# Attention shares: one VectorE multiply over spread reciprocals in place of four scalings on two engines

## The chip, the cores and the metric

The kernel runs on one core of a Trainium2 chip. The metric is the device time of one execution in microseconds; lower is better.

## What is computed

The reference is a chain of three layers in float32 over 4 sequences of 576 tokens:

- attention with 8 heads of 64, a causal window of 128 keys and a distance bias: `scores = scale * q k^T + bias`, then `attn = exp(scores - max)`, `attn = attn / (sum(attn) + 1e-9)`, `out = attn v`;
- a feed-forward layer with layer norm: `x + relu(norm(x) * g_ln @ w_ch1) @ w_ch2`, 512 to 2048 to 512;
- a gated layer with a convolution over three tokens: `h = relu(x @ w_in)`, `h * sigmoid(conv(h)) @ w_out`, 512 to 1024 to 512.

The change touches the division of `attn` by its sums. All weights arrive as 64-bit floats and are turned into float32 parts on the chip.

## The kernel before, in words

The work has an attention stage, whose order is written out by hand, and everything after it, whose order a planner in the program (`Plan`, lines 24 to 210) makes from due times and costs. The change touches the attention stage alone.

Attention works on 72 tiles (two pairs of sequences, four pairs of heads, nine tiles of 128 queries), each with two heads. A step of the code handles a pair of tiles, so four score blocks of 128 x 128; there are 36 pairs. The loop at line 835 takes two pairs, `a` and `b`, a round, 18 rounds in all. Each engine runs its instructions in the order in which the loop writes them, and semaphores tie the engines together. What a pair passes through:

- `scores` (line 692): TensorE, into PSUM. Each query tile sees two key tiles.
- `join` and `minima` (lines 720 and 726): VectorE, a masked copy (L724) that lays the two key tiles' halves over each other, and a minimum per row (L728). Both read PSUM.
- `exponentials` (line 730): ScalarE, four calls (L738), each also writing its row's sum into `sm`.
- `shares` (line 743): VectorE adds 1e-9 to the four sums (L746) and takes reciprocals (L747), and then the four 128 x 128 blocks of `pp` are scaled in place (L750). Blocks 0 and 2 are done by VectorE, blocks 1 and 3 by GpSimd.
- `turn_p` (line 755): four TensorE transposes of `pp` into PSUM (L760).
- `copy_p` (line 762): ScalarE copies them to SBUF (L765).
- `select_p` (line 768): GpSimd makes the parts of the two key tiles, two selects of 128 x 512 (L772).
- `values` (line 777): TensorE multiplies with `v` (L788), and `outputs` (line 793) copies the result out.

In a round the VectorE queue holds: join and minima of `a`, join and minima of `b`, `shares(b - 4)`, the extras of the even half round, `shares(a)`, the extras of the odd one. GpSimd's holds: `select_p(b - 8)`, its part of `shares(b - 4)`, extras, its part of `shares(a)`, `select_p(a - 4)`, extras.

The extras (`extras`, line 817) are mostly the conversion of the first twelve feed-forward weight blocks (`weights_step`, line 373; `FINE_START` and `FINE_AT` say when): a rescale on GpSimd (L341), three integer steps on VectorE (L349, L354, L359), a copy on ScalarE (L388) and a subtraction on VectorE (L391). By their half rounds L354 falls between the two `shares` of a round, and L391, L359 and L349 behind the second. A few rounds also carry a layer norm's steps, among them four subtractions on GpSimd (L483). Behind the loop the last pairs are drained with their own written order (lines 894 to 917).

Of the kernel before, what the change touches and what calls it, by code (L numbers as in the profile page):

```python
# [14 lines left out]
ALU = mybir.AluOpType  # L15
PSUM = bass.MemoryType.PSUM

P = 128
# [176 lines left out]
def tile_kernel(  # L195
# [28 lines left out]
    V, S, G, T = nc.vector, nc.scalar, nc.gpsimd, nc.tensor  # L224
# [288 lines left out]
    with ExitStack() as actx:  # L513
# [110 lines left out]
        def blhs_f(kind: int, a: int = 0):  # L624
            return blhs[:, kind, a:].bitcast(F32)

        V.tensor_scalar(
            out=blhs[:, 0, :], in0=cf[:, P:W], scalar1=er[0], scalar2=er[1], op0=ALU.mult, op1=ALU.add
        )
        V.tensor_scalar(out=cb[:, 3:4], in0=er[0], scalar1=-1.0, scalar2=None, op0=ALU.mult)  # L630
        for i, r, base in ((1, 2, 3), (2, 3, 3), (0, 4, 1)):
            V.scalar_tensor_tensor(
                out=cb[:, i : i + 1], in0=er[r], scalar=BIG, in1=cb[:, base : base + 1],
                op0=ALU.mult, op1=ALU.add,
            )
        for i in range(4):
            cs = slice(i * D, (i + 1) * D)
            V.tensor_scalar(
                out=b0[:, cs], in0=cf[:, cs], scalar1=er[1], scalar2=cb[:, i : i + 1],
                op0=ALU.mult, op1=ALU.add,  # L640
            )
        for kind, r in ((1, 2), (3, 4)):
            V.tensor_scalar(
                out=blhs[:, kind, :], in0=blhs_f(0), scalar1=er[r], scalar2=None, op0=ALU.add
# [3 lines left out]
            out=blhs[:, 2, TAIL:], in0=blhs_f(0, TAIL), scalar1=er[2], scalar2=er[3],  # L648
            op0=ALU.add, op1=ALU.add,
        )  # L650
        for pr in range(NPAIR):
            V.tensor_scalar(
                out=brhs[:, pr, :], in0=b0, scalar1=sl[:, pr : pr + 1], scalar2=None, op0=ALU.mult
# [89 lines left out]
        def shares(n: int):  # L743

            sm = live["sm", n]
            V.tensor_scalar(out=sm[:, 1], in0=sm[:, 0], scalar1=1e-9, scalar2=None, op0=ALU.add)  # L746
            V.reciprocal(out=sm[:, 1], in_=sm[:, 1])  # L747
            pp = live["pp", n].rearrange("p u h j -> p (u h) j")
            for i in range(4):
                (G if i % 2 else V).tensor_scalar(  # L750
                    out=pp[:, i, :], in0=pp[:, i, :], scalar1=sm[:, 1, i : i + 1], scalar2=1.0,
                    op0=ALU.mult, op1=ALU.mult,
                )

        def turn_p(n: int, pool=ps_t, tag="pt"):
            pp = live.pop(("pp", n))
# [78 lines left out]
        for n in range(0, NS, 4):  # L835
# [21 lines left out]
            if n > 4:  # L857
                shares(b - 4)
# [4 lines left out]
            exponentials(a)  # L863
            exponentials(b, range(2 if 0 < n and not last else 4))
            shares(a)
            if not before:
                shares(b)
# [1006 lines left out]
```

## Time and profile before

| what | value |
|---|---|
| time, median of 3 runs | 740.08 us (736.44 to 740.39) |
| the profiled execution | 737.25 us, of which its span is 735.6 us |
| PE, DVE, ACT, POOL busy in the span | 97%, 73%, 55%, 30% |
| attention stage | from the start to about 148 us |

PE is TensorE, PEld its weight loads, DVE VectorE, ACT ScalarE, POOL GpSimd, SP SyncE; L750 is line 750 of the kernel. Busy time of an engine is a union of its instructions' recorded times. On VectorE the recorded time of one instruction runs some 0.08 us into that of the next, so the distance from start to start is what an instruction takes of the queue.

### The profile page before, as it was taken

The numbers are of one execution on the slowest core, as the hardware profiler recorded it, in microseconds if no ns is written. First come the engines' busy times: TensorE is split into PE (matmuls) and PEld (weight loads), VectorE is DVE, ScalarE is ACT, GpSimd is POOL, SyncE is SP. The second block draws the span as 40 slices with busy tenths as digits, with TensorE's granted clock in tenths as the row PEclk, the third lists the DMA queues.
The fourth block names the chain that finished last, engine by engine and source line by source line (L and its number), as shares of the span: only waits on it lengthen the run. The fifth ranks groups of instructions, "written<-read, shape, count | busy, mean of one in ns | idle before, by whom it ended". The sixth has DMA issues, their size and how long they took to land.

```text
span 735.6 us, 13436 instructions
## 1 busy us (share of the span) xinstructions
PE 711.3 (97%) x4704; PEld 664.1 (90%) x4704; DVE 534.2 (73%) x1073; ACT 404.4 (55%) x1050; POOL 223.3 (30%) x388
## 2 busy tenths in 40 slices
PE   7999998899999999999999999999999999999998
PEld 6777776799889999999999999999999898998887
DVE  6899999578899845655678765568369988787630
ACT  4888877635444323333436333344377787776741
POOL 1778789635542312321210233243421000000000
PEclk9999999999999999999999999999999999999999
DMA  6877765226859714987870599997832000000011
GB/s 152 185 180 175 199 159 144 71 86 201 241 164 336 260 52 121 290 256 247 244 225 25 155 283 296 297 270 227 255 93 80 16 16 29 29 30 15 29 53 48
DMA packets 122302, 114.62 MB, mean 156 GB/s; under 512 B 63552, under 2 KB 87292, under 8 KB 122236
## 3 DMA queue, kind: packets, MB, share of 16 engines
q1 hardware_dynamic: 101020, 76.81, 35.1%
q0 software_dynamic: 20160, 36.71, 18.5%
q8 instruction: 37, 0.61, 0.3%
q10 hardware_dynamic: 1056, 0.26, 0.2%
q14 instruction: 29, 0.24, 0.1%
HBM read 80.70 MB, written 33.05 MB: 155 GB/s over the span
## 4 chain that ended last, share of the span: by engine, by line
PE 67%; DVE 2%; DMA 1%; ACT 1%; POOL 1%; issue 0%; SPq 0%; ACTq 0%
PE bank L1008 66%; DMA fa<-in_moe_w_out 1%; DVE fa L978 1%; DMA fa<-in_moe_w_ch 1%; PE bank L1055 1%; DVE fa L986 0%; POOL r L1183 0%; ACT fa L971 0%; DVE fa L359 0%; DVE x L978 0%; ACT fa L339 0%; DVE h L1698 0%; DVE fa L354 0%; ACT L971 0%; POOL small L1077 0%
## 5 line engine op out<-in xcount | busy, mean ns | idle before, releaser
L1008 PE MATMUL bank<-hhr,r 128*128 128x384 f32 x1152 | 214.8, 338 | 2.9 <-DVE hhr L986 1.0
L1008 PE MATMUL bank<-r,r 128*128 128x288 f32 (+1 forms) x1248 | 203.9, 314 | 1.6 <-DVE fa L978 0.9
L1008 PEld LDWEIGHTS bank<-hhr,r 128*128 128x128 f32 x1152 | 198.7, 188 | 5.3 <-POOL r L1183 1.6
L1008 PEld LDWEIGHTS bank<-r,r 128*128 128x128 f32 x1248 | 194.0, 188 | 4.4 <-ACT fa L971 1.4
L1279 POOL DMA_DIRECT2D r<-w1d x96 | 51.4, 536 | 164.7 <-PE bank L1008 146.8
L971 ACT ACTIVATE fa<-bank 128x288 f32<-128x288 f32 (+1 forms) x112 | 49.9, 445 | 67.4 <-PE bank L1008 65.5
L1008 PE MATMUL bank<-r 128*128 128x512 f32 (+2 forms) x360 | 80.7, 369 | 0.0
L1008 PEld LDWEIGHTS bank<-r 128*128 128x128 f32 x360 | 64.1, 188 | 9.0
L1008 PE MATMUL bank<-xn,r 128*128 128x384 f32 x360 | 67.3, 336 | 0.0
L971 ACT ACTIVATE r<-fa 128x256 fp32r<-128x256 f32 (+2 forms) x94 | 47.7, 521 | 33.0 <-DVE fa L359 11.5
L1008 PEld LDWEIGHTS bank<-xn,r 128*128 128x128 f32 x360 | 62.8, 188 | 0.0
L971 ACT ACTIVATE hhr<-bank 128x384 fp32r<-128x384 f32 x46 | 22.5, 490 | 73.1 <-PE bank L1008 73.1
L978 DVE TENSOR_TENSOR fa<-bank,fa 128x288 f32<-128x288 f32 (+1 forms) x88 | 43.5, 500 | 24.3 <-ACT fa L971 14.4
L738 ACT ACTIVATE pp<-ps,mn 128x128 f32<-128x128 f32 x144 | 51.3, 380 | 13.1 <-DVE mn L728 9.6
L750 POOL TENSOR_SCALAR pp<-pp,sm 128x128 f32<-128x128 f32 x72 | 43.2, 611 | 32.8 <-DVE sm L747 31.6
L986 DVE SCALAR_TENSOR_TENSOR fa<-fa,cw 128x576 f32<-128x576 f32 x64 | 51.2, 813 | 1.5 <-ACT fa L971 0.7
L978 DVE TENSOR_TENSOR r<-fa,r 128x256 fp32r<-128x256 f32 (+1 forms) x74 | 37.6, 521 | 16.7 <-ACT r L971 13.4
L772 POOL TENSOR_SCALAR_AFFINE_SELECT pt<-pc 128x512 f32<-128x512 f32 x72 | 46.9, 680 | 1.7 <-ACT pc L765 1.4
L713 PE MATMUL ps<-kt,qt 64*128 64x256 f32 x288 | 43.9, 399 | 2.5 <-ACT pp L738 1.7
L788 PE MATMUL po<-pt,rawv 128*64 128x128 f32 x544 | 38.4, 283 | 6.9 <-POOL pt L772 4.4
L1008 PE MATMUL bank<-r,hhr 128*128 128x512 f32 (+1 forms) x192 | 44.5, 381 | 0.0
L788 PEld LDWEIGHTS po<-pt,rawv 128*64 128x64 f32 x544 | 29.5, 138 | 15.5 <-POOL pt L772 12.2
(136 smaller groups left out, 1062.4 us busy)
## 6 DMA issues: line engine op xcount, KB each, us to landing
r<-w1d POOLq DMA_DIRECT2D x96, 256.0 KB, 4.8
fa<-in_moe_w_ch SPq DMA_DIRECT2D x32, 512.0 KB, 4.6
w1d<-r SPq DMA_DIRECT2D x40, 256.0 KB, 3.3
wind<-r SPq DMA_DIRECT2D x28, 256.0 KB, 4.1
r<-wind POOLq DMA_DIRECT2D x28, 256.0 KB, 4.2
out<-h SPq DMA_DIRECT2D x17, 256.0 KB, 2.0
rawq<-in_q SPq DMA_DIRECT2D x32, 128.0 KB, 3.8
rawv<-in_v SPq DMA_DIRECT2D x32, 128.0 KB, 3.0
```

What stands on the lines that cost most here:

```text
L713: T.matmul(ps[:, h, u, :].rearrange("p (o j) -> p o j", o=2), lhs, rhs, start=i == 0, stop=i == 1,)
L738: S.activation(pp[:, u, h, :], sc[:, h, u], AF.Exp, bias=mn[:, h, u : u + 1], scale=-1.0, accum_out=sm[:, 0, i : i + 1],)
L750: (G if i % 2 else V).tensor_scalar(out=pp[:, i, :], in0=pp[:, i, :], scalar1=sm[:, 1, i : i + 1], scalar2=1.0, op0=ALU.mult, op1=ALU.mult,)
L772: G.affine_select(out=parts[:, i], in_=pc, compare_op=ALU.is_ge, fill=0.0, base=base, pattern=[[0, 4], [sign, P]], channel_multiplier=-sign,)
L788: T.matmul(po[h * D : (h + 1) * D, u, :], rvs[bl, pr][:, t - 1 + i, h, :], pt[:, i, 2 * u + h, :], start=i == i0, stop=i == 1,)
L971: "S", ns + 90 * isinstance(scale, bass.AP), lambda: S.activation(out, src, func, **kw),
L978: "V", tt_ns(cols(out)), lambda: V.tensor_tensor(out=out, in0=a, in1=b, op=op),
L986: lambda: V.scalar_tensor_tensor(out=out, in0=a, scalar=sc, in1=b, op0=op0, op1=op1),
L1008: T.matmul(out, lhs, rhs, start=start and n == 0, stop=stop and n == len(items) - 1, skip_group_check=True,)
L1055: T.transpose(px[:, c, :], xs[c], ident)
L1279: plan.add("G", 1100, lambda: nc.gpsimd.dma_start(dst, src), [src], [dst], nbytes=262144)
```

## The change

In `shares` the loop of four scalings is replaced by one VectorE multiply over all four blocks, 128 x 512. Its second operand is the row of four reciprocals, each read 128 times by a step of zero. GpSimd has no part in `shares` any more. The sums, the reciprocals and everything else stay.

```diff
             V.tensor_scalar(out=sm[:, 1], in0=sm[:, 0], scalar1=1e-9, scalar2=None, op0=ALU.add)
             V.reciprocal(out=sm[:, 1], in_=sm[:, 1])
             pp = live["pp", n].rearrange("p u h j -> p (u h) j")
-            for i in range(4):
-                (G if i % 2 else V).tensor_scalar(
-                    out=pp[:, i, :], in0=pp[:, i, :], scalar1=sm[:, 1, i : i + 1], scalar2=1.0,
-                    op0=ALU.mult, op1=ALU.mult,
-                )
+            r = sm[:, 1].rearrange("p (i o) -> p i o", o=1).broadcast_to([P, 4, P])
+            V.tensor_tensor(out=pp, in0=pp, in1=r, op=ALU.mult)
```

## Rows read from the trace of the kernel before

**Rows 1.** Windows: stretch, length; busy time and count per engine; clock; DMA share, GB/s.

```profile
core 0 of [0], span 735.6 us
...
27.59:131.23 103.64, 96.83 (x1006) 77.87 (x1006) 97.19 (x226) 85.60 (x344) 85.08 (x134) 0.98 0.69 168
131.23:147.84 16.61, 14.35 (x142) 11.72 (x139) 8.46 (x22) 9.26 (x31) 10.22 (x18) 1.00 0.25 78
147.84:213.13 65.29, 62.05 (x362) 60.15 (x361) 55.51 (x89) 31.18 (x59) 31.87 (x31) 1.00 0.56 167
```

**Rows 2.** Chain that ended last, in order of time: start us, us, what.

```profile
213.13 4.09 PE bank L1008 x22
```

**Rows 3.** Groups on VectorE up to 143 us: count, busy us, mean ns, idle before.

```profile
L750 DVE TENSOR_SCALAR pp<-pp,sm 128x128 f32<-128x128 f32 x72 | 25.5, 396 | 1.3
...
L746 DVE TENSOR_SCALAR sm<-sm 128x4 f32<-128x4 f32 x36 | 7.0, 195 | 1.8 <-ACT pp L738 1.8
L349 DVE TENSOR_SCALAR fa<-fa 128x512 int32<-128x512 int32 x12 | 6.8, 566 | 0.6 <-POOL fa L341 0.6
```

**Rows 4.** Groups on GpSimd up to 143 us, the same columns.

```profile
L772 POOL TENSOR_SCALAR_AFFINE_SELECT pt<-pc 128x512 f32<-128x512 f32 x72 | 46.9, 680 | 1.7 <-ACT pc L765 1.4 <-PE po L788 0.4
L750 POOL TENSOR_SCALAR pp<-pp,sm 128x128 f32<-128x128 f32 x72 | 43.2, 611 | 32.8 <-DVE sm L747 31.6 <-ACT kt L814 0.5 <-ACT pc L765 0.4
```

**Rows 5.** Waits of VectorE from 27 to 143 us: total us, times, longest.

```profile
DVE ps L724 <- PE ps L713: 3.6, 6, 1.2
DVE fa L349 <- POOL fa L341: 0.6, 1, 0.6
```

**Rows 6.** Waits of TensorE up to 143 us.

```profile
PE po L788 <- POOL pt L772: 4.4, 6, 1.3
```

**Rows 7.** Timeline of VectorE in one round: start us, us, instruction, count.

```profile
65.07 0.60 DVE L750 TENSOR_SCALAR pp<-pp,sm 128x128 f32<-128x128 f32 x2
65.59 0.70 DVE L354 SCALAR_TENSOR_TENSOR fa<-fa 128x512 int32<-128x512 int32 x1
66.22 0.26 DVE L746 TENSOR_SCALAR sm<-sm 128x4 f32<-128x4 f32 x1
...
66.72 0.87 DVE L750 TENSOR_SCALAR pp<-pp,sm 128x128 f32<-128x128 f32 x2
67.52 0.70 DVE L391 TENSOR_TENSOR r<-fa,r 128x512 fp32r<-128x512 f32 x1
68.13 0.77 DVE L359 SCALAR_TENSOR_TENSOR fa<-fa 128x512 int32<-128x512 int32 x1
```

**Rows 8.** Timeline of GpSimd in the same round.

```profile
65.14 1.31 POOL L750 TENSOR_SCALAR pp<-pp,sm 128x128 f32<-128x128 f32 x2 [1.29 <-DVE sm L747]
...
67.48 1.92 POOL L750 TENSOR_SCALAR pp<-pp,sm 128x128 f32<-128x128 f32 x2
69.36 1.22 POOL L772 TENSOR_SCALAR_AFFINE_SELECT pt<-pc 128x512 f32<-128x512 f32 x2
```

**Rows 9.** Timeline of ScalarE in the same round.

```profile
65.58 0.62 ACT L765 ACTIVATE pc<-ptp 128x512 f32<-128x512 f32 x1
```

**Rows 10.** Line views of L391, L746, L349: shortest/median/longest ns, first and last start.

```profile
L391 DVE TENSOR_TENSOR r<-fa,r x12: 684/700/702, 39.5 to 136.8; 128x512 fp32r<-128x512 f32 x12
...
L746 DVE TENSOR_SCALAR sm<-sm x36: 136/162/353, 12.7 to 137.5; 128x4 f32<-128x4 f32 x36
...
L349 DVE TENSOR_SCALAR fa<-fa x12: 414/514/855, 26.2 to 122.1; 128x512 int32<-128x512 int32 x12
```

**Rows 11.** Timeline of VectorE at 117 us.

```profile
117.03 0.35 DVE L746 TENSOR_SCALAR sm<-sm 128x4 f32<-128x4 f32 x1
```

**Rows 12.** Timeline of GpSimd at 116 us.

```profile
116.71 1.24 POOL L772 TENSOR_SCALAR_AFFINE_SELECT pt<-pc 128x512 f32<-128x512 f32 x2
```

**Rows 13.** Timeline of GpSimd behind the loop.

```profile
136.46 1.23 POOL L750 TENSOR_SCALAR pp<-pp,sm 128x128 f32<-128x128 f32 x2 [0.89 <-DVE sm L747]
...
138.85 0.71 POOL L750 TENSOR_SCALAR pp<-pp,sm 128x128 f32<-128x128 f32 x2
139.53 1.22 POOL L772 TENSOR_SCALAR_AFFINE_SELECT pt<-pc 128x512 f32<-128x512 f32 x2
```

## The prediction

> **What bounds the kernel now.** I read the windows first. From 27.59 to 131.23 us, fourteen rounds of the attention loop, VectorE is busy 97.19 of 103.64 us and GpSimd 85.08 [rows 1]. TensorE shows 96.83, but a busy matmul record is no proof of pace, so I asked what VectorE waits for: 3.6 us for scores and 0.6 us for a rescale in that stretch and up to 143 us [rows 5]. VectorE is the bound of the loop, with some 4 us of slack in it. TensorE's own waits for the selects, 4.4 us [rows 6], are what makes the scores late for VectorE.
>
> The chain that ended last starts only behind attention, in the weight conversion, and joins TensorE at 213.13 us [rows 2]. From 147.84 on the next stage needs PSUM and SBUF that attention frees, and TensorE is busy 62.05 of its 65.29 us [rows 1]. So a microsecond at attention's end is a microsecond of the total, in either direction.
>
> **What is removed and added.** 72 VectorE scalings of 396 ns and 72 GpSimd scalings of 611 ns go [rows 3, 4]; 36 VectorE multiplies of 128 x 512 come. No DMA moves, and no queue of SP is passed.
>
> *VectorE's own time.* The multiply has no row. The nearest is L391: same engine, 512 elements, two operands in SBUF, 684 to 702 ns [rows 10]. The far end above is 855 ns, the longest L349, a 512-element step that was held by GpSimd [rows 10]; the near end below is 684. I take 700, since all twelve L391 lie there, though the operand with a step of zero is in no row. From start to start that is 0.62 us (67.52 to 68.13 is 0.61 [rows 7]). The pair that goes takes 2 x 396 ns less two overlaps of 80 ns, 0.63 us. In a quiet round it is 0.52 (65.07 to 65.59), in a held one 0.80 (66.72 to 67.52) [rows 7]. 36 x (0.62 - 0.63) = **-0.4 us** (at 684 ns -0.9, at 855 ns +5.2).
>
> *GpSimd's time.* 43.2 us of its 85 to 100 go. Not one microsecond of that is gain by itself: GpSimd idled 31.6 us before these scalings, waiting for the reciprocals [rows 4]. The value lies in what its selects do earlier. That has a good side and a bad side.
>
> *Steps that GpSimd holds up today.* L746 and L349 are VectorE steps with one SBUF source, and the trace shows them held while GpSimd works. The L746 at 117.03 us took 0.35 us, under a pair of selects that began at 116.71 [rows 11, 12], where the shortest took 136 ns [rows 10]. Against median and shortest, the means cost 36 x (195 - 162) = 1.2 us and 12 x (566 - 414) = 1.8 us [rows 3, 10]. Together 3.0 us that could go: **-3.0**.
>
> *The new holds.* In the round shown, ScalarE ends `copy_p(a - 4)` at 65.58 + 0.62 = 66.20 [rows 9], but its selects start at 69.36, since two scalings of 1.92 us stand ahead [rows 8]. There they run beside the joins, which read PSUM. After the change GpSimd is free, and they start about 66.3, a tenth behind the copy. The second L746 of the round started at 66.22 [rows 7], and comes a tenth later behind the longer multiply, at 66.32. If the select is first, L746 waits for most of it, about 0.5 of 0.68 us (estimate from the mean of L772 [rows 4] less the tenth in which it starts), with the reciprocal, the multiply, L391 and the next join queued behind. This can happen only where an L354 lies between the two `shares`, twelve rounds. Bounds: 0 and 12 x 0.5 = 6.0 us. The two starts lie within some hundredths in this round, and where ScalarE is later than here L746 is through first; between the bounds I take a third of the rounds, four: **+2.0**. L349 at the round's end meets the same selects: two-operand steps ahead of it stall GpSimd (1.92 us for two scalings that were 0.71 together behind the loop [rows 8, 13]), so a select is still under way when L349 comes. Bounds 0 and 855 - 414 = 0.44 us, twelve times, 5.3 us; I take 0.3: **+3.6**.
>
> *Waits for scores.* Earlier selects let `values` start earlier, and the scores behind it. Of 4.2 us [rows 5] I take half: **-2.0** (0 to -4.2).
>
> *The drain behind the loop.* GpSimd's queue loses 1.23 and 0.71 us there [rows 13], but the new multiplies stall its selects for 0.6 us each, and a held L746 delays the last multiply. Bounds 0 and -1.9; I take **-0.5**.
>
> Sum: -0.4 - 3.0 + 2.0 + 3.6 - 2.0 - 0.5 = **-0.3 us**. The profiled execution, 737.25 us (span 735.6), would be about 737.0; it lies 2.8 us under the median, so I carry the difference to the median: 740.08 - 0.3 = **739.8 us**. About 0.5%, 3.7 us, is what a measurement of this kernel can tell from no change.
>
> **A rule against it.** The trace shows all twelve L391 within 18 ns of each other, with GpSimd busy four fifths of the time [rows 1, 10]: a two-operand step of VectorE was never held there, and GpSimd paid instead [rows 8]. The Trainium skill, page "SBUF — State Buffer", section "Who interferes with whom", says that a VectorE instruction with two SBUF inputs contends with a GpSimd instruction that reads SBUF, and that issue order decides who blocks. By that the multiply would wait for a select that began first; it stands below as a rival, and the trace speaks against that half of it.
>
> **The rivals.**
>
> *Faster: GpSimd's relief comes through.* The early selects fall beside steps that read PSUM, and new holds do no more than today's. Then -3.0 is cancelled by as much and no more, and the waits of VectorE go whole: -0.4 - 4.2 - 0.5 = -5.1, **735.0 us**. For it: GpSimd is busy 85.08 of 103.64 us now [rows 1], and TensorE's 4.4 us behind the selects [rows 6] are as much as VectorE's own waits. Against: VectorE has no other slack to give.
>
> *Slower: the selects meet the short steps every round.* The mechanism of the new holds at its upper ends: the second L746 held in all twelve rounds (6.0) and L349 each time by 0.44 (5.3): -0.4 - 3.0 + 6.0 + 5.3 - 2.0 - 0.5 = +5.4, **745.5 us**. It decides at one point: whether the first select starts before or behind 66.32 in such a round. For it: a round that VectorE stretches gives ScalarE time, so `copy_p` is punctual more often. Against: in the round shown it is a matter of hundredths.
>
> *Slower: the multiply is held by selects.* Selects fill 46.9 of 143 us [rows 4], a third. A multiply that meets one would wait half of 0.68 us: 36 x 0.33 x 0.34 = 4.0 us, **743.8 us**. The rule of the Trainium skill, "SBUF — State Buffer", section "Who interferes with whom", would bring it about. Against it stand the twelve L391.
>
> *The change doesn't do what it says*: the step-of-zero operand is read at a lower rate. At 855 ns it is +5.6 against my sum, 745.4. No row speaks for it.
>
> **How the numbers follow.** No change that can be told: 0.46 (own range 736.4 to 743.8). Faster rival: 0.28. Held short steps: 0.17; held multiply: 0.07; slow operand: 0.02. So faster 0.28, same 0.46, slower 0.26. The range reaches from the faster case to near the slower one, 735 to 745 us; it leaves out the full sum of all gains (-0.4 - 3.0 - 4.2 - 1.9 = -9.5) and the upper ends together.
>
> **What would show it.** In the changed profile L750 should be one VectorE group, x36, near 700 ns, with no GpSimd rows; above 750 ns would mean held multiplies or a slow operand. L772 should start about 0.1 us behind L765 instead of 3 us. Holds show as L746's and L349's means: I expect about 195 to 220 ns and 700 ns; an L746 mean over 300 ns is the slower rival, both at 162 and 414 ns the faster one. VectorE's waits for scores should be half of 3.6 us. The first start of L339 behind attention says what the stage gained. The forecast is wrong if that moves by over 3.7 us either way.

## The result: slower by 1.4%, and the profile after

The changed kernel takes 749.16 us (median of 4 runs, 746.35 to 750.94) beside 738.42 us for the kernel before (736.44 to 740.39): ratio 1.014, 95% interval 1.0116 to 1.0164. The forecast was no change, 739.8 us in a range of 735 to 745.

The page of the profiled execution (747.73 us) gives the span and the engines' busy times. GpSimd lost 31 of its 223 us, and VectorE, which was to stay nearly as it was, gained 13.

```profile
span 746.0 us, 13315 instructions
## 1 busy us (share of the span) xinstructions
PE 711.8 (95%) x4704; PEld 666.7 (89%) x4704; DVE 547.0 (73%) x1037; ACT 404.1 (54%) x1050; POOL 192.6 (26%) x316
```

The same fourteen rounds of the attention loop, from the first join of round 4 to that of round 18, in the windows view (length; busy time and count of PE, PEld, DVE, ACT, POOL; clock, DMA):

```profile
27.44:140.63 113.19, 98.78 (x1038) 80.87 (x1036) 108.53 (x197) 86.09 (x344) 61.56 (x80) 0.97 0.63 154
```

They took 103.64 us before [rows 1]: 9.55 us of the 10.4 by which the span grew (735.6 to 746.0) lie here. In the chain that ended last TensorE's long run starts at 223.86 us, where it stood at 213.13 [rows 2], and keeps that distance to the end. TensorE's granted clock in the loop is 0.97, where it was 0.98; that isn't what lengthened the loop, since VectorE waited less for TensorE than before (the waits are shown below, with the prediction's terms).

```profile
223.86 4.09 PE bank L1005 x22
```

Now the groups on VectorE up to 153 us (count, busy us, mean ns, idle before), then those on GpSimd. Lines behind 750 are three lower than before: L769 is the select.

```profile
L750 DVE TENSOR_TENSOR pp<-pp,sm 128x512 f32<-128x512 f32 x36 | 27.8, 771 | 1.2
...
L391 DVE TENSOR_TENSOR r<-fa,r 128x512 fp32r<-128x512 f32 x12 | 12.1, 1007 | 0.0
L359 DVE SCALAR_TENSOR_TENSOR fa<-fa 128x512 int32<-128x512 int32 x12 | 11.5, 959 | 0.0
L349 DVE TENSOR_SCALAR fa<-fa 128x512 int32<-128x512 int32 x12 | 9.4, 782 | 0.0
L354 DVE SCALAR_TENSOR_TENSOR fa<-fa 128x512 int32<-128x512 int32 x12 | 8.6, 721 | 0.0
L746 DVE TENSOR_SCALAR sm<-sm 128x4 f32<-128x4 f32 x36 | 8.3, 232 | 1.6 <-ACT pp L738 1.6
...
L425 DVE SCALAR_TENSOR_TENSOR xn<-xm,gain,xn 128x384 fp32r<-128x384 f32 x4 | 3.1, 808 | 0.0
```

```profile
L769 POOL TENSOR_SCALAR_AFFINE_SELECT pt<-pc 128x512 f32<-128x512 f32 x71 | 56.2, 815 | 66.4 <-ACT pc L762 63.9 <-PE po L785 2.5
```

In the kernel before, the groups on VectorE that [rows 3] leaves out read:

```profile
L359 DVE SCALAR_TENSOR_TENSOR fa<-fa 128x512 int32<-128x512 int32 x12 | 9.0, 752 | 0.0
L354 DVE SCALAR_TENSOR_TENSOR fa<-fa 128x512 int32<-128x512 int32 x12 | 8.4, 701 | 0.0
L391 DVE TENSOR_TENSOR r<-fa,r 128x512 fp32r<-128x512 f32 x12 | 8.4, 697 | 0.0
...
L425 DVE SCALAR_TENSOR_TENSOR xn<-xm,gain,xn 128x384 fp32r<-128x384 f32 x4 | 2.3, 622 | 0.0
```

The multiply is the smaller part of what grew: 27.8 us against 25.5 for the scalings [rows 3]. Unheld it takes 693 ns, as its line view shows (shortest/median/longest), so the operand with a step of zero isn't slow:

```profile
L750 DVE TENSOR_TENSOR pp<-pp,sm x36: 691/693/1128, 12.9 to 148.7; 128x512 f32<-128x512 f32 x36
```

The steps around it grew more: L391, which the change does not touch, went from 697 to 1007 ns in the mean, L359 from 752 to 959. GpSimd, which used to idle 31.6 us waiting for reciprocals [rows 4], now idles 63.9 us waiting for ScalarE's copies: its selects start as soon as a copy is there.

What that does stands in the timeline of one round, VectorE first (start us, us, instruction), then GpSimd:

```profile
69.95 1.14 DVE L354 SCALAR_TENSOR_TENSOR fa<-fa 128x512 int32<-128x512 int32 x1
71.02 0.59 DVE L746 TENSOR_SCALAR sm<-sm 128x4 f32<-128x4 f32 x1
...
71.86 0.86 DVE L750 TENSOR_TENSOR pp<-pp,sm 128x512 f32<-128x512 f32 x1
72.64 0.68 DVE L391 TENSOR_TENSOR r<-fa,r 128x512 fp32r<-128x512 f32 x1
73.24 1.11 DVE L359 SCALAR_TENSOR_TENSOR fa<-fa 128x512 int32<-128x512 int32 x1
74.28 0.85 DVE L349 TENSOR_SCALAR fa<-fa 128x512 int32<-128x512 int32 x1
```

```profile
69.71 0.84 POOL L341 TENSOR_SCALAR fa<-fa 128x512 f32<-128x512 f32 x1 [2.85 <-DMA fa<-in_moe_w_ch]
70.55 1.63 POOL L769 TENSOR_SCALAR_AFFINE_SELECT pt<-pc 128x512 f32<-128x512 f32 x2
72.82 2.03 POOL L769 TENSOR_SCALAR_AFFINE_SELECT pt<-pc 128x512 f32<-128x512 f32 x2 [0.65 <-ACT pc L762]
```

The rescale begins at 69.71, before L354 at 69.95, and L354 takes 1.14 us instead of 0.70. The pair of selects begins at 70.55, and the four-element L746 takes 0.59. L391 at 72.64 is ahead of the select of 72.82 and takes its 0.68; the select then gets in behind it, and L359 takes 1.11 and L349 0.85. Whoever is first has the operands. The line view of L391 shows it over all twelve (shortest/median/longest ns): it is either free, near 676 ns, or held by 0.44 us.

```profile
L391 DVE TENSOR_TENSOR r<-fa,r x12: 676/1114/1121, 41.4 to 146.8; 128x512 fp32r<-128x512 f32 x12
```

### The profile page after: what moved, and what is told of

Read it like the earlier page. It is cut to its first block, busy times and chain, and to the rows that moved or that the text cites. A ratio compares the mean times of both kernels' runs of the same rounds, so it can differ in the third digit from the quotient of the medians.

```text
span 746.0 us, 13315 instructions
## 1 busy us (share of the span) xinstructions
PE 711.8 (95%) x4704; PEld 666.7 (89%) x4704; DVE 547.0 (73%) x1037; ACT 404.1 (54%) x1050; POOL 192.6 (26%) x316
## 4 chain that ended last, share of the span: by engine, by line
PE 67%; DVE 2%; POOL 1%; ACT 1%; DMA 1%; issue 0%; ACTq 0%; SPq 0%
PE bank L1005 67%; DVE fa L975 1%; DMA fa<-in_moe_w_ch 1%; PE bank L1052 1%; POOL r L1180 0%; DVE fa L983 0%; ACT fa L968 0%; DVE x L975 0%; DVE fa L359 0%; DVE h L1695 0%; ACT L968 0%; POOL small L1074 0%; DVE hhr L1486 0%; ACT fa L339 0%; DVE r L1738 0%
## 5 line engine op out<-in xcount | busy, mean ns | idle before, releaser
L769 POOL TENSOR_SCALAR_AFFINE_SELECT pt<-pc 128x512 f32<-128x512 f32 x72 | 56.8, 812 | 66.4 <-ACT pc L762 63.9
L713 PE MATMUL ps<-kt,qt 64*128 64x256 f32 x288 | 47.0, 420 | 2.6 <-ACT pp L738 1.7
L983 DVE SCALAR_TENSOR_TENSOR hhr<-bank,hhr 128x384 fp32r<-128x384 f32 x46 | 25.4, 551 | 21.5 <-ACT hhr L968 21.3
L968 ACT ACTIVATE fa<-fa 128x576 f32<-128x576 f32 (+1 forms) x64 | 38.8, 620 | 3.1 <-DVE fa L975 1.9
L1005 PEld LDWEIGHTS bank<-r,hhr 128*128 128x128 f32 x192 | 34.0, 188 | 6.8
```

Source lines behind the costliest of these rows:

```text
L713: T.matmul(ps[:, h, u, :].rearrange("p (o j) -> p o j", o=2), lhs, rhs, start=i == 0, stop=i == 1,)
L769: G.affine_select(out=parts[:, i], in_=pc, compare_op=ALU.is_ge, fill=0.0, base=base, pattern=[[0, 4], [sign, P]], channel_multiplier=-sign,)
L968: "S", ns + 90 * isinstance(scale, bass.AP), lambda: S.activation(out, src, func, **kw),
L983: lambda: V.scalar_tensor_tensor(out=out, in0=a, scalar=sc, in1=b, op0=op0, op1=op1),
L1005: T.matmul(out, lhs, rhs, start=start and n == 0, stop=stop and n == len(items) - 1, skip_group_check=True,)
```

## The experiments

Theory S: the change frees GpSimd's queue, its selects start about 2 to 3 us earlier in a round, and now they run beside VectorE's steps on SBUF instead of beside the joins, which read PSUM; each VectorE step that finds a GpSimd instruction ahead of it waits for that one. Rival M: the wide multiply, with two operands in SBUF, is what costs. Every run below stands against runs of the kernel before on the same chip. The loop's time is that of the fourteen rounds above, in the one profiled execution of each version.

| version | ratio to before (95%) | loop, us |
|---|---|---|
| the kernel before | 1 | 103.64 |
| the change | 1.014 (1.0116 to 1.0164) | 113.19 |
| e1: before, GpSimd's scalings left out | 1.0043 (1.0023 to 1.0063) | 106.99 |
| e2: change, idle scalings back on GpSimd | 1.0079 (1.005 to 1.0108) | 108.94 |
| e3: four scalings, all on VectorE | 1.0141 (1.0108 to 1.0174) | 115.12 |
| e4: change, selects behind a latch | 1.0019 (0.9998 to 1.004) | 103.59 |
| e5: change, rescales on ScalarE | 1.0139 (1.011 to 1.0169) | 111.69 |
| e6: e4 with rescales on ScalarE | 1.0128 (1.0099 to 1.0157) | 109.63 |
| e7: before, rescales on ScalarE | 1.0149 (1.0127 to 1.017) | 108.99 |
| e8: change, each select in four | 1.0076 (1.0056 to 1.0097) | 108.61 |
| e9: e4, each rescale in four | 1.0035 (1.002 to 1.005) | 103.81 |
| e11: e4, last round in the change's order | 1.0052 (1.0029 to 1.0075) | 104.52 |

### e1: take the GpSimd work away and nothing else

```diff
-            for i in range(4):
-                (G if i % 2 else V).tensor_scalar(
+            for i in (0, 2):
+                V.tensor_scalar(
```

> The kernel before with GpSimd's two scalings of a pair left out (blocks 1 and 3 of pp stay unscaled); VectorE's two stay, nothing is added to VectorE. Theory S (the selects start earlier, because GpSimd's queue no longer holds them back, and hold VectorE's SBUF steps): slower than before although work is gone, 742 to 749 us, with L391 and L359 above 850 ns in the mean. Rival M (the wide multiply itself is what costs): no slower than before, 734 to 739 us, L391 near 697 ns.

Measured: 742.47 us against 739.37, slower by 0.43%. A kernel that lacks 72 instructions and has nothing new is slower than the one that has them. VectorE's groups, then a stretch of its timeline and of GpSimd's:

```profile
L391 DVE TENSOR_TENSOR r<-fa,r 128x512 fp32r<-128x512 f32 x12 | 10.8, 901 | 0.0
L359 DVE SCALAR_TENSOR_TENSOR fa<-fa 128x512 int32<-128x512 int32 x12 | 9.9, 825 | 0.0
```

```profile
68.86 1.13 DVE L391 TENSOR_TENSOR r<-fa,r 128x512 fp32r<-128x512 f32 x1
69.92 1.11 DVE L359 SCALAR_TENSOR_TENSOR fa<-fa 128x512 int32<-128x512 int32 x1
70.95 0.85 DVE L349 TENSOR_SCALAR fa<-fa 128x512 int32<-128x512 int32 x1
```

```profile
68.23 1.22 POOL L772 TENSOR_SCALAR_AFFINE_SELECT pt<-pc 128x512 f32<-128x512 f32 x2
69.79 1.74 POOL L772 TENSOR_SCALAR_AFFINE_SELECT pt<-pc 128x512 f32<-128x512 f32 x2 [0.34 <-ACT pc L765]
```

The selects of 68.23 stand ahead of L391, the next pair ahead of L359 and L349, with no wide multiply anywhere. M expected no loss and falls as the whole cause. (L359's mean, 825 ns, is under the 850 that S expected.) The loop lost 3.35 us here and 9.55 in the change, so early selects alone are not the whole sum either: the change also has a multiply that contends with GpSimd, so its selects are drawn out (815 ns in the mean, 719 here) and are ahead of more steps. This last is a reading of the traces; no run isolates it.

### e3: no wide multiply, no GpSimd

```diff
-                (G if i % 2 else V).tensor_scalar(
+                V.tensor_scalar(
```

> All four scalings on VectorE as four 128 x 128 steps, none on GpSimd. Theory S: slow like the change, 747 to 756 us, since GpSimd is as free as there and each short step can be held by a select. Rival M: the wide two-operand form is gone, so 739 to 744 us (36 x some 0.15 us more of VectorE than before).

Measured: 749.81 us, as slow as the change and as S expected, and above M's range. The loss here isn't all holds, because this version gives VectorE plain work as well. Four scalings that nothing holds take 0.88 us:

```profile
62.34 0.88 DVE L750 TENSOR_SCALAR pp<-pp,sm 128x128 f32<-128x128 f32 x4
```

A pair took 25.5 / 36 = 0.71 us before [rows 3], so 36 x 0.17 = 6.1 us of the 10.4 are the added work (an estimate from these two rows, near the price in M's expectation). The other 4 us are left for holds: L746's mean is 289 ns up to 150 us, where it was 195 before, and L391's 758. So the run speaks against M, by these 4 us and not by the whole loss.

### e2: put the GpSimd time back without the work

```diff
             V.tensor_tensor(out=pp, in0=pp, in1=r, op=ALU.mult)
+            for i in (1, 3):
+                G.tensor_scalar(
+                    out=spare[:, i // 2, :], in0=ident, scalar1=sm[:, 1, i : i + 1], scalar2=1.0,
+                    op0=ALU.mult, op1=ALU.mult,
+                )
```

> The changed kernel with GpSimd's two scalings put back at their old places as idle work: they read a constant tile and the reciprocals and write a spare tile. Theory S: the selects are late again, and the time comes back to 737 to 743 us, L391 under 750 ns. Rival M: 748 to 752 us, as nothing is taken from VectorE.

Measured: 743.73 us in the median of 9 runs, just above what S expected. Six of them took 742.22 to 743.73 us, three 747.73 to 748.88. Idle work on GpSimd makes the change faster, which M has no room for, but only by about half. The profiled execution is the slowest of the nine, as slow as the change, and of the 11.6 us that its span has over the kernel before only 5.3 lie in the loop; so it can't explain the median. It shows which holds are left: the selects are late again, but the rescales, which stood between the scalings before as well, are now ahead of L391 and L359. L391's mean there is 968 ns, and S had expected under 750: that part was missed.

```profile
71.02 1.16 DVE L391 TENSOR_TENSOR r<-fa,r 128x512 fp32r<-128x512 f32 x1
```

```profile
70.46 1.17 POOL L341 TENSOR_SCALAR fa<-fa 128x512 f32<-128x512 f32 x1
```

So S has to be said more widely: a 512-element rescale ahead of a VectorE step does it as a select does.

### e4: leave the change, move the selects back beside the joins

The first pair of selects of a round goes to the start of the next round, behind a one-column GpSimd step that reads what VectorE wrote last in the round.

```diff
+                G.tensor_scalar(
+                    out=latch, in0=last_v[0], scalar1=1.0, scalar2=1.0, op0=ALU.mult, op1=ALU.mult
+                )
+                select_p(a - 8)
                 copy_p(b - 8)
                 select_p(b - 8)
...
                 copy_p(a - 4)
-                select_p(a - 4)
+                if last:
+                    select_p(a - 4)
```

> The changed kernel with the first two selects of a round moved to the start of the next round, behind a one-column GpSimd step that waits for VectorE's last step of the round; so they run beside the joins. Theory S: L391 and L359 under 800 ns, and faster than before, 731 to 739 us. Rival M: 745 us or more.

Measured: 741.08 us against 739.37 in the same series, ratio 1.0019 (0.9998 to 1.004). The wide multiply is still there, and the loop takes 103.59 us, as before the change. VectorE's groups (L392, L360, L350 are L391, L359, L349 of before; L355 is L354), and GpSimd's timeline of one round:

```profile
L355 DVE SCALAR_TENSOR_TENSOR fa<-fa 128x512 int32<-128x512 int32 x12 | 10.3, 857 | 0.0
L750 DVE TENSOR_SCALAR sm<-sm 128x4 f32<-128x4 f32 x36 | 9.2, 256 | 1.3 <-ACT pp L742 1.3
L392 DVE TENSOR_TENSOR r<-fa,r 128x512 fp32r<-128x512 f32 x12 | 8.6, 719 | 0.0
L360 DVE SCALAR_TENSOR_TENSOR fa<-fa 128x512 int32<-128x512 int32 x12 | 8.2, 684 | 0.0
...
L350 DVE TENSOR_SCALAR fa<-fa 128x512 int32<-128x512 int32 x12 | 5.0, 419 | 0.0
```

```profile
62.16 0.19 POOL L848 TENSOR_SCALAR latch<-fa 128x1 f32<-128x1 f32 x1 [3.60 <-DVE fa L350]
62.30 2.40 POOL L774 TENSOR_SCALAR_AFFINE_SELECT pt<-pc 128x512 f32<-128x512 f32 x4
66.13 0.97 POOL L342 TENSOR_SCALAR fa<-fa 128x512 f32<-128x512 f32 x1 [1.43 <-DMA fa<-in_moe_w_ch]
```

Four selects run in 2.40 us beside the joins, whose masked copies stay at 683 to 697 ns, and the three steps at the round's end are back at 719, 684 and 419 ns. This is the run that settles the cause: the placement of GpSimd's instructions against VectorE's, with every other part of the change kept, brings the loop back, where M expected 745 us or more. What remains are the rescales (66.13), which now meet L355 and L750. It was expected to beat the kernel before and does not: the loop is level, but the drain behind it, from the last round's join to the first weight step, takes 19.19 us (131.28 to 150.47) where it took 16.51 (131.23 to 147.74). What lengthened it stands under e9 and e11.

### e8: the same selects in smaller pieces

```diff
-                G.affine_select(
-                    out=parts[:, i], in_=pc, compare_op=ALU.is_ge, fill=0.0, base=base,
-                    pattern=[[0, 4], [sign, P]], channel_multiplier=-sign,
-                )
+                for q in range(4):
+                    G.affine_select(
+                        out=parts[:, i, q], in_=pc[:, q], compare_op=ALU.is_ge, fill=0.0, base=base,
+                        pattern=[[sign, P]], channel_multiplier=-sign,
+                    )
```

> The changed kernel with each select of 128 x 512 cut into four of 128 x 128, same work, same place in the queue. If a VectorE step is held for the one GpSimd instruction in front of it, and not for the whole row of them: L391 and L359 under 800 ns and 740 to 746 us. If the hold is set by how long GpSimd is busy in all: 749 us or more, since GpSimd's selects take longer in pieces.

Measured: 743.93 us against 738.75, half of the loss gone, although GpSimd's selects take 91.4 us in all in place of 56.8. The line views of L391 and of the select (here L770):

```profile
L391 DVE TENSOR_TENSOR r<-fa,r x12: 685/772/1143, 40.5 to 142.3; 128x512 fp32r<-128x512 f32 x12
```

```profile
L770 POOL TENSOR_SCALAR_AFFINE_SELECT pt<-pc x288: 285/288/835, 19.6 to 150.4; 128x128 f32<-128x128 f32 x144
```

L391's median is 87 ns above its shortest, where it was 438 above in the change. A VectorE step waits for the one GpSimd instruction ahead of it, not for the row of them, and the shorter that is, the shorter the wait: 0.09 us for a select whose shortest time is 0.285, and 0.44 in the change, where it is 0.63. That explains the kernel before: in [rows 7, 8] GpSimd's scaling of 67.48 is a 128-element piece, L391 beside it is not held, and L359 behind takes 0.77 us, 0.09 over its shortest.

### e5, e6, e7: the rescales on ScalarE

```diff
-                    rescale(t, raw, G)
+                    rescale(t, raw, S)
```

> The changed kernel with the twelve rescales (L341, 128 x 512) moved from GpSimd to ScalarE, selects left where they are. If the selects do most of the holding: 743 to 749 us, L391 still above 850 ns. If the rescales do as much as the selects: 738 to 743 us.

> The version with the selects behind the latch, and the rescales on ScalarE as well, so nothing of GpSimd but the layer norm's steps can hold VectorE. Theory S: L354 near 690 ns and L746 near 165 ns in the mean, 733 to 738 us, under the kernel before. If ScalarE waits for weights at the head of its queue instead: 738 to 743 us.

> Control: the kernel before with the rescales on ScalarE. Its selects run beside the joins already, so theory S expects little, 736 to 741 us, with L750 on VectorE still near 390 ns because GpSimd's own scalings come between.

Measured: 747.89, 747.83 and 748.86 us against 738.75. With selects left early (e5) L391 is 1044 ns, and VectorE is busy 105.22 us in the loop, against 108.53 in the change and 97.19 before: the selects do most of the holding. The time of e5 alone, in its expected range, wouldn't show it, since the move itself costs as much (e7). In e6 VectorE has what S wanted, L746 at 188 ns, L391 at 720, though L354 still at 819, and still loses: ScalarE's queue now waits for weights, and exponentials wait behind. e7 shows that this price has nothing to do with the change. ScalarE's wait for weights in e6 (us in all, times, longest):

```profile
ACT fa L340 <- DMA fa<-in_moe_w_ch: 12.8, 7, 3.0
```

GpSimd's queue waited 11.0 us for these transfers in e4, and the loop there is level with the kernel before; ScalarE's queue has no such room. How much of the price is this wait isn't separated: ScalarE's own work in e7's loop grew as well, from 85.60 to 90.95 us, by as much as the loop. The expectations of e6 (733 to 738, or 738 to 743) and e7 (736 to 741) were missed; the second branch of e6 named the wait, at half the size of the loss.

### e9 and e11: what is left in the latch version

e9 cuts each rescale into four of 128 x 128; e11 keeps the change's own select order in the loop's last round (and takes the latch off there).

> The version with the selects behind the latch, and each rescale of 128 x 512 on GpSimd cut into four of 128 x 128. If what is left of the holds there is the length of the one rescale in front of a VectorE step: L746 under 230 ns and L354 under 800 ns in the mean (256 and 857 with whole rescales), and 736 to 740 us. If the pieces hold as much in sum: 740 to 743 us, no different from the whole ones.

> The version with the selects behind the latch, but the last round of the loop keeps the change's own order, so the drain behind the loop is not delayed by the latch. In the latch version's profile the drain (last round's start to the first L339 step behind attention) took 18.8 us, in the kernel before 16.5, in the change 17.3. If the latch costs the drain that difference: 1 to 2 us less than the latch version's 741.1, so 738.5 to 740.5 us, the same as the kernel before within its uncertainty. If the held select in the last round costs as much: 740.5 to 743 us.

Measured: e9 740.73 us, ratio 1.0035; L354 fell from 857 to 716 ns as expected and L746 from 256 to 235 (under 230 was expected), but L391 rose from 719 to 820 and the multiply to 760: four pieces hold about as much in sum as one whole, spread over more steps. e11 743.0 us, ratio 1.0052, above its range: its drain takes 19.11 us, no less than with the latch, so the latch in the last round was not what lengthened it. (Counted from the joins of their own profiles, the latch version's drain is 19.2 us and the change's 17.5, a little over the figures in that expectation.) What lengthened it is in the kept traces. The drain of e9 has the same order as e4's and takes 17.51 us, like the change's 17.50. The difference is one group of `values` multiplications on TensorE, first in e4, then in e9:

```profile
140.93 3.63 PE L790 MATMUL po<-pt,rawv 128*64 128x128 f32 x32
```

```profile
142.51 1.97 PE L793 MATMUL po<-pt,rawv 128*64 128x128 f32 x32
```

TensorE's granted clock was 0.53 over the first of these stretches, so at the lower of its two levels (1.2 of 2.4 GHz) for nearly all of it, and 1.00 over the second. In e11 it was 0.60 over the same group, which took 3.11 us. In e4 and e9 alike TensorE had stood idle for 2.06 us shortly before, with only four transposes between, so why the clock fell in one and not in the other stays open, and so does how often it does: each version has one profile. No version tried beats the kernel before.

## Why the prediction was wrong

- **What bounds the kernel**: right. VectorE bounds the loop, and the loop's 9.55 us and the drain's 1.0 went into the total undiminished.
- **VectorE's own time**, -0.4 us: the price of the multiply was right when free (median 693 ns, 700 taken), but its mean is 771, as some were held. Per pair 771 - 80 ns in place of 2 x 396 - 160: 36 x 59 ns = +2.1 us.
- **Steps held today and new holds**, -3.0 + 2.0 + 3.6 = +2.6 us: right in place and nearly in size. L746 cost 36 x (232 - 195) = 1.3 us more than before and L349 12 x (782 - 566) = 2.6, together +3.9.
- **Waits for scores**, -2.0 us: right in the number, but that proves little of the mechanism. The forecast let scores come earlier; here VectorE itself came later, by 9.55 us over the loop, which gives TensorE time by itself. VectorE's waits from 27 us on fell from 4.2 to 2.2 us:

```profile
DVE ps L724 <- PE ps L713: 2.2, 5, 0.7
```

- **The drain**, -0.5 us: wrong sign, +1.0 (16.51 to 17.50); the held steps there belong to the sums in this list.
- **The step that failed** is the sentence "a two-operand step of VectorE was never held there, and GpSimd paid instead". It was read from twelve L391 at 684 to 702 ns beside a GpSimd that was busy four fifths of the time. Busy was not the point: what stood ahead of L391 then was a 128-element scaling, and the 512-element selects came later, beside the joins. So L391, L359, L354 and L425 had no term in the sum. They cost 3.7 + 2.5 + 0.2 + 0.8 = +7.2 us.

The rows together give 2.1 + 3.9 + 7.2 - 2.0 = +11.2 us, against 10.4 in the span; where the 0.8 us between them went isn't shown.

L391 took 676 ns when it was first and 1114 when a select was. The Trainium skill, page "SBUF — State Buffer", section "Who interferes with whom", says that a VectorE instruction with two SBUF inputs contends with a GpSimd instruction that reads SBUF, and that issue order decides; the trace agrees in both. The rival of the held multiply, which the prediction built on this, had a chance of 0.07 and was priced for the multiply alone, +4.0 us, though the change moved the selects against every two-operand step of the round; the multiply got +2.1, its neighbours +7.2. The rival of the held short steps named the place and the deciding point (the selects' start behind the copy), but left out the same neighbours.

## What to carry to other kernels

Where VectorE bounds, GpSimd's instructions have a place as well as a length: beside the joins, which read PSUM, they cost nothing here (e4), beside steps on SBUF each held the next VectorE step, the longer the instruction the more (0.09 us for 128 elements, 0.44 for 512). Work taken from GpSimd moves everything behind it in its queue, so ask which VectorE steps that will then meet, and keep the old place with a small dependency if it was a good one. "Never held in the trace of before" is evidence only for the instructions that were ahead there, at the size they had.

## What the runs showed of the hardware

- A 512-element GpSimd instruction that is ahead holds a 512-element VectorE step with two SBUF operands by 0.44 us (L391, 1114 ns against 676), and a four-element step with one by up to 0.46 (L746, 601 against 136); a 128-element select holds L391 by about 0.09 (e8).
- A GpSimd instruction that waits behind a VectorE step gets in before the next one, even when VectorE's steps follow without a gap: the select recorded from 72.82 us let L391 finish and then held L359 (1.11 us).
- The masked copies of the joins, which read PSUM, took 683 to 697 ns with GpSimd's selects beside them (e4); a select did not hold them.
- Leaving 72 GpSimd instructions out, with nothing added, made the kernel slower by 0.43% (e1).
- 32 `values` multiplications of the drain took 3.63 us at a granted clock of 0.53 and 1.97 at 1.00 (e4, e9).
